# A gated mix of two attentions on one core: the first scores ahead of the last projected tile, and one PSUM layout for both parts

## The chip, the core and the metric

The kernel runs on one core of a Trainium2 chip. The metric is the device time of one execution in microseconds (us). Engines are named as the profile names them: PE (TensorE matmul), PEld (its weight loads), DVE (VectorE), ACT (ScalarE), POOL (GpSimd) and SP (SyncE, which issues nearly all DMAs). All lines (L…) are those of the kernel before, unless the kernel after is named.

## What is computed

With `x` of 2048 rows and 448 columns, 16 heads of 28, and two sets of weights:

```python
g = sigmoid((x * gate_w).sum(-1, keepdims=True))
# A: sliding window, 8 keys, 2 apart, per head
kg = k[:, :, idx_c, :]; vg = v[:, :, idx_c, :]
logits = einsum("bhsd,bhswd->bhsw", q, kg) * scale        # masked, softmax over w
a = (softmax(logits) weighted sum of vg) @ A_wo
# B: full attention, 16 heads
p = softmax(einsum("bhqd,bhkd->bhqk", q, k) * 28 ** -0.5)
b = einsum("bhqk,bhkd->bhqd", p, v) @ B_wo
return g * a + (1 - g) * b
```

All is float32. The kernel splits each matmul operand into a high and a low part and sums three products.

## The kernel before, in words

**Part one, the projections** (from the start to about 252.7 us). 92 tiles, written out in a list, give q, k, v of both attentions. From tile 10 on a tile is summed in two halves of 64 contraction rows, which run side by side on PE, into the two halves of one PSUM tile `PJ[n % 2]` (L289); ACT copies both halves out (L362), POOL adds them (L363). Between the products stand matmuls of another kind, `s1_half` (L155): they work out full score rows, of which DVE keeps only the row maximum (L162), because the softmax of B needs the maximum before its exponentials. Each of tiles 12 to 91 carries four of them, into `PM[0]` and `PM[1]`, and gives four of the 1024 maxima.

**Part two, attention B with attention A beside it** (about 252.7 to 788 us) is a loop of 256 steps: 16 units (4 head groups by 4 blocks of 512 queries) of 16 key tiles. A step does, in this order on PE:

- `scores` (L1016): twelve matmuls for four heads (three products each), in tokens like `"10"` (bank 1, product 0). While maxima are left, three matmuls for maxima stand between them (`s0`, `s1`, `s2`, L144). `s0` goes into `T1`, `s1` and `s2` into a pair of banks. DVE reduces `T1` to one maximum and the pair to two (L148).
- ACT takes the exponential of two heads at a time, two instructions a step (L1044).
- `do_av` (L992) of the **previous** step: four matmuls of exponentials with V into `av` (L995), summed over the 16 key tiles of a unit.

The order on each engine is the order in which the program is written, with its waits set by a recording layer from the tiles that instructions read and write. One step later than a unit's last `do_av`, `fin_copy` (L852) has ACT copy `av` out to `osb` (L854). In step 0 no `do_av` is due, and two matmuls on idle data stand in its place (L1116).

Into the steps go, by lists with due steps and costs (L685 to L755), the instructions of attention A: POOL does its products, DVE its reductions (L626, L637, L647) and transposes (L674), ACT eight exponentials (`L`, L642). When a unit's 64 maxima are there, `max_parts` (DVE, ACT, POOL; L172), two steps later `max_turn` (DVE, L186) and `max_store` (SP) put them into DRAM, from where `load_q` (L119) reads them as two more rows of the next queries.

**The end.** After step 234 no maxima are left, and 92 pieces of the output projection (L838) are spread over steps 235 to 255; the rest follows.

**PSUM.** Part one holds four tiles `PS[0..3]` of two banks each (r0 to r3; the numbers 128, 132, 136, 140 in the rows below). At the change to part two this pool is closed and three tiles T0 to T2 of two banks, and two separate tiles of one bank, `T1` and `av`, are taken in the same place (L532 to L537).

Of the kernel before, what the change touches and what calls it, by code (L numbers as in the profile page):

```python
# [25 lines left out]
def gated_mix_kernel(ctx: ExitStack, tc: tile.TileContext, xT, xn, gw, wA, wB, woAB, out):  # L26
# [24 lines left out]
    tctx = [ExitStack()]  # L51
    PS = [tctx[0].enter_context(tc.tile_pool(name=f"ps{i}", bufs=1, space=bass.MemoryType.PSUM)).tile(
        [128, 2, 512], F32, name=f"r{i}") for i in range(4)]
    PJ, PM = PS[0:2], PS[2:4]
    T = []

    def banks(n):
        for i in range(n):
            pool = ctx.enter_context(tc.tile_pool(name=f"t{i}", bufs=1, space=bass.MemoryType.PSUM))
            T.append(pool.tile([128, 2, 512], F32, name=f"T{i}"))  # L60

# [144 lines left out]
    with tc.tile_pool(name="xp", bufs=1) as xp, tc.tile_pool(name="wp", bufs=2) as wp:  # L206
# [77 lines left out]

        def product(n, p, half, first, last):
# [3 lines left out]
            bank = PS[n % 4][:, 0, :] if half is None else PJ[n % 2][:, half, :]  # L289
# [38 lines left out]

        fini = []
# [9 lines left out]
        def qk_tile(n, nb, rows):  # L339
# [8 lines left out]
            nc.scalar.activation(raw, PJ[n % 2], AF.Copy)  # L348
# [10 lines left out]
        def add_halves(n, dst, gate=None):  # L359
            raw = pair("raw")  # L360
            cols = D + 2 * (gate is not None)
            nc.scalar.activation(raw[:, :, 0:cols], PJ[n % 2][:, :, 0:cols], AF.Copy)  # L362
# [88 lines left out]
        for n, t in enumerate(tiles):  # L451
# [77 lines left out]
    tctx[0].close()  # L529
    pctx.close()  # L530
    pm = ctx.enter_context(tc.tile_pool(name="pm", bufs=8))
    banks(3)  # L532
    RP = T[2], T[0]
    TP = T[1]
    pool = ctx.enter_context(tc.tile_pool(name="psv", bufs=1, space=bass.MemoryType.PSUM))
    T1 = pool.tile([128, 512], F32, name="T1")
    av = pool.tile([128, 512], F32, name="av")  # L537

# [155 lines left out]
    for c in range(8):  # L696
# [28 lines left out]
        for i in range(4):  # L725
            item("dve", c0 + 53 + 0.1 * i, ("t", c, i), 0.43 if c < 7 else 0.35, [(("a", c, W - 1, 1), 1), (("t", c, i - 1), 0)],
# [275 lines left out]
    ALONE = "10 20 30 00 11 21 31 01 12 22 32 02".split()  # L1002
# [13 lines left out]
    def scores(u, kt, cur):  # L1016
# [10 lines left out]
        for tok in WITH if k else ALONE:  # L1027
            if tok[0] == "s":
# [49 lines left out]
    for u in range(NU):  # L1078
        g, b = divmod(u, NB)
        for kt in range(NJ):  # L1080
            st = NJ * u + kt
            if kt == (8 if u < 12 else 12) and u + 1 < NU:
                load_q(u + 1)
# [16 lines left out]
            if finished:  # L1100
# [5 lines left out]
                lag = 2 if v < NU - 1 else 1  # L1106
# [3 lines left out]
            issue("act", st, 0)  # L1110
# [3 lines left out]
            else:  # L1114
                for _ in range(2):
# [68 lines left out]
```

## Time and profile before

| what | value |
|---|---|
| median of 3 runs | 905.44 us (905.26 to 906.26) |
| the profiled execution's own time | 906.4 us |
| its span from first to last instruction | 904.6 us |
| PE busy | 897.4 us (99%) |
| DVE, ACT, POOL busy | 735.3, 646.1, 633.7 us |
| granted TensorE clock | 1.00 |

A row of the timeline reads: start, length, engine, line, operation, tile written and tiles read, how many instructions are merged in it, and in brackets the idle time of the engine ahead of it with what ended that. A row of the groups reads: line, engine, operation, tiles and shapes, count, then busy time and mean of one in ns, then idle time ahead and who ended it. Matmul records start when a matmul enters the array, and their ends are modelled, so PE shows as busy throughout.

### The profile page before, as it was taken

Reading aid. Unit: us, or ns where it says so; the run is one execution under the profiler, and the core shown is the slowest. Engines: PE = TensorE matmul, PEld = TensorE weight load, DVE = VectorE, ACT = ScalarE, POOL = GpSimd, SP = SyncE. Lnnn points to the kernel's source line nnn. Section 1 sums busy time; section 2 is a strip of 40 time slices with the busy share of each in tenths; the row PEclk is TensorE's granted clock in tenths of the full one; section 3 lists DMA queues with packets and bytes.
Section 4 is the critical chain, followed back from the end, with each engine's and each line's share of the span. In section 5 each row is a group of like instructions: output and inputs, shape, how many; then the busy total and the mean of one; then the engine's idle time right before and its main releaser. Section 6 shows DMA issues by size and latency. Waiting matters only on the chain.

```text
span 904.6 us, 20583 instructions
## 1 busy us (share of the span) xinstructions
PE 897.4 (99%) x8334; PEld 534.2 (59%) x8334; DVE 735.3 (81%) x989; ACT 646.1 (71%) x775; POOL 633.7 (70%) x502
## 2 busy tenths in 40 slices
PE   9999999999999999999999999999999999999998
PEld 6899999999944444444444444444444444466667
DVE  6488999999989999999999999999999888610012
ACT  6456434443378898898989889888889898855550
POOL 2489847464479799998989999899999389500100
PEclk9999999999999999999999999999999999999999
DMA  9887403554362341245144421523122413455333
GB/s 269 289 264 194 142 12 84 145 133 121 96 245 65 98 119 54 81 108 130 27 120 122 113 89 42 141 66 79 48 82 55 134 26 103 126 155 146 91 95 102
DMA packets 113838, 104.29 MB, mean 115 GB/s; under 512 B 74628, under 2 KB 82180, under 8 KB 112960
## 3 DMA queue, kind: packets, MB, share of 16 engines
q1 hardware_dynamic: 113600, 102.72, 40.2%
q8 instruction: 65, 1.06, 0.5%
q10 hardware_dynamic: 144, 0.26, 0.1%
q14 instruction: 29, 0.24, 0.1%
HBM read 61.99 MB, written 40.48 MB: 113 GB/s over the span
## 4 chain that ended last, share of the span: by engine, by line
PE 92%; POOL 4%; ACT 1%; DVE 1%; DMA 0%; issue 0%; SPq 0%; ACTq 0%; DVEq 0%; POOLq 0%
PE T L1041 28%; PE av L995 26%; PE r L298 15%; PE T L838 8%; PE r L293 8%; PE r L144 5%; PE T L144 4%; POOL oat L670 1%; POOL prod L665 1%; ACT P L1044 1%; DMA raw<-in_wB 0%; POOL prod L616 0%; DVE MX L148 0%; SPq L220 0%; POOL prod L621 0%
## 5 line engine op out<-in xcount | busy, mean ns | idle before, releaser
L1044 ACT ACTIVATE P<-T 128x1024 f32<-128x1024 f32 x512 | 497.2, 1025 | 92.2 <-PE T L1041 91.0
L148 DVE TENSOR_REDUCE MX<-T 128x1 f32<-128x512 f32 x470 | 440.1, 952 | 22.4 <-PE T L144 10.3
L995 PE MATMUL av<-P,V 128*32 128x512 f32 x2048 | 272.7, 605 | 0.4 <-ACT osb L854 0.3
L1041 PEld LDWEIGHTS T<-QH,KH 30*128 30x128 f32 x1024 | 90.6, 181 | 221.4 <-ACT P L1044 196.9
L144 PE MATMUL T<-KH,QP 28*128 28x512 f32 x704 | 219.4, 454 | 0.3 <-DVE MX L162 0.3
L162 DVE TENSOR_REDUCE MX<-r 128x2 f32<-128x1024 f32 x160 | 192.6, 1220 | 24.7 <-PE r L144 23.1
L1041 PE MATMUL T<-QH,KH 30*128 30x512 f32 x1024 | 210.9, 489 | 1.0 <-DVE MX L148 0.8
L1041 PE MATMUL T<-QH,KL 28*128 28x512 f32 x1024 | 185.8, 397 | 0.0
L1041 PE MATMUL T<-QL,KH 28*128 28x512 f32 x1024 | 182.9, 392 | 0.0
L616 POOL TENSOR_TENSOR prod<-qt,kt 128x896 f32<-128x896 f32 x64 | 135.5, 2120 | 0.2
L362 ACT ACTIVATE raw<-r 128x896 f32<-128x896 f32 (+1 forms) x64 | 58.9, 920 | 97.9 <-PE r L298 96.6
L670 POOL TENSOR_TENSOR oat<-oat,prod 128x896 f32<-128x896 f32 x56 | 118.2, 2110 | 2.7
L144 PEld LDWEIGHTS T<-KH,QP 28*128 28x128 f32 x704 | 86.0, 181 | 27.6 <-ACT P L1044 20.9
L363 POOL TENSOR_TENSOR ast<-raw 128x448 f32<-128x448 f32 x48 | 55.4, 1154 | 58.2 <-ACT raw L362 45.8
L665 POOL TENSOR_TENSOR prod<-vt,L 128x896 f32<-128x896 f32 x56 | 95.5, 1705 | 0.6
L1041 PEld LDWEIGHTS T<-QL,KH 28*128 28x128 f32 x1024 | 93.2, 184 | 0.0
L1041 PEld LDWEIGHTS T<-QH,KL 28*128 28x128 f32 x1024 | 91.7, 183 | 1.0
L144 PE MATMUL r<-KH,QP 64*128 64x512 f32 x320 | 86.7, 390 | 0.0
L995 PEld LDWEIGHTS av<-P,V 128*32 128x32 f32 x2048 | 40.3, 108 | 78.1 <-issue 73.1
L298 PE MATMUL r<-wh,xh 64*128 64x448 f32 (+1 forms) x512 | 85.4, 362 | 0.0
L298 PE MATMUL r<-wh,xl 64*128 64x448 f32 (+1 forms) x384 | 70.0, 363 | 0.0
L298 PE MATMUL r<-wl,xh 64*128 64x448 f32 (+1 forms) x448 | 66.1, 367 | 0.0
(120 smaller groups left out, 1038.1 us busy)
## 6 DMA issues: line engine op xcount, KB each, us to landing
a_scr<-ast SPq DMA_DIRECT2D x24, 448.0 KB
qk_hi<-qkh SPq DMA_DIRECT2D x24, 256.0 KB
qk_lo<-qkh SPq DMA_DIRECT2D x24, 256.0 KB
rbc<-rs SPq DMA_DIRECT2D x60, 64.0 KB
QP<-qk_hi SPq DMA_DIRECT2D x64, 56.0 KB
KL<-qk_lo SPq DMA_DIRECT2D x16, 224.0 KB
QH<-qk_hi SPq DMA_DIRECT2D x64, 56.0 KB
QL<-qk_lo SPq DMA_DIRECT2D x64, 56.0 KB
```

Of the source, the lines that this page charges most:

```text
L144: nc.tensor.matmul(bank, qhis[u][h % 2][r, 128 * qs:128 * qs + 128], KH[u // NB % 3][r, 512 * kc:512 * kc + 512], start=True, stop=True)
L148: r = nc.vector.tensor_reduce(MX[:, n % NMX:n % NMX + k], bank, axis=X, op=ALU.max)
L162: nc.vector.tensor_reduce(m, PM[k], axis=X, op=ALU.max)
L293: nc.tensor.matmul(bank, ws[c][rows, k, t[4]:t[4] + 128], x, start=first, stop=last)
L298: nc.tensor.matmul(bank[:, 0:cols], x, ws[c][rows, k, 0:cols], start=first, stop=last)
L616: nc.gpsimd.tensor_tensor(out=p, in0=qt[c], in1=kvt["k", c % 2][:, HALO - DIL * w:HALO - DIL * w + NJ, :], op=ALU.mult)
L665: nc.gpsimd.tensor_tensor(out=dst, in0=kvt["v", c % 2][:, HALO - DIL * w:HALO - DIL * w + NJ, :].rearrange("p j (h d) -> p j h d", d=DH), ...
L670: nc.gpsimd.tensor_tensor(out=oat[c], in0=oat[c], in1=oat[c, w], op=ALU.add)
L838: writes(bank, nc.tensor.matmul(bank[:, :D], src, wo[c][:, k, :], start=(first and k == ks[0] and i == 0), stop=(last and k == ks[-1] and ...
L995: nc.tensor.matmul(av[32 * h:32 * h + 32, :], V[:, kt, 4 * g + h, :], tiles_[h], start=(kt == 0), stop=(kt == NJ - 1), skip_group_check=True)
L1041: nc.tensor.matmul(bank[a], (KH[g % 3], KH[g % 3], KL[g % 2])[t][r, ks], (qh, ql, qh)[t][r, :], start=(t == 0), stop=(t == 2))
L1044: e = nc.scalar.activation(p, RP[0] if a == "2" else mine, AF.Exp, scale=SCALE).ins
```

## The change

The four tiles `PS[0..3]` now stay for both parts. `RP` is `PS[2]` and `PS[1]`, `TP` is `PS[3]`; **`T1` and `av` are the two halves of `PS[0]`**. The last projected tile (91) goes to `PS[3]` and carries no matmuls for maxima, so that `PS[2]` and `PS[1]` are free for the twelve score matmuls and two exponentials of step 0, which are issued ahead of it (`first_scores`). Four maxima more are left for part two, in steps 1 to 236; the output pieces are spread over steps 237 to 255. Step 0 has no score matmuls, no maxima and no idle matmuls any more. Further: `max_turn` four steps after `max_parts` instead of two; A's transposes of its last two chunks a step later; A's exponentials not in the first three steps of units 0 to 11; the queries of the last unit loaded at the 15th key tile rather than the 13th; a pair of maxima that would wrap around the store `MX` is reduced in two pieces.

```diff
-    tctx = [ExitStack()]
-    PS = [tctx[0].enter_context(tc.tile_pool(name=f"ps{i}", bufs=1, space=bass.MemoryType.PSUM)).tile(
+    PS = [ctx.enter_context(tc.tile_pool(name=f"ps{i}", bufs=1, space=bass.MemoryType.PSUM)).tile(
         [128, 2, 512], F32, name=f"r{i}") for i in range(4)]
     PJ, PM = PS[0:2], PS[2:4]
...
+    RP, TP = (PS[2], PS[1]), PS[3]
+    T1, av = PS[0][:, 0, :], PS[0][:, 1, :]
...
+        def joint(n):
+            return TP if n == len(tiles) - 1 else PJ[n % 2]
...
+        def first_scores():
+            qh, ql = Qs[0]
+            for tok in ALONE:
+                h, t = int(tok[0]), int(tok[1])
+                r = slice(32 * h, 32 * h + (DH + 2 if t == 0 else DH))
+                bank = RP[h in (0, 3)][:, h in (0, 2), :]
+                nc.tensor.matmul(bank, (KH[0], KH[0], KL[0])[t][r, 0:128], (qh, ql, qh)[t][r, :],
+                                 start=(t == 0), stop=(t == 2))
+                if t == 2 and h in (0, 2):
+                    p = pair(f"P{h}")
+                    nc.scalar.activation(p, RP[h == 0], AF.Exp, scale=SCALE)
+                    cur0[(h + 3) % 4], cur0[h] = p[:, 0, :], p[:, 1, :]
...
+            if n == len(tiles) - 1:
+                first_scores()
             if n < FULL:
                 project(n)
             else:
-                project_halves(n, [S1_START <= m < S1_START + 80 for m in (n, n + 1)])
+                project_halves(n, [S1_START <= m < len(tiles) - 1 for m in (n, n + 1)])
...
-    banks(3)
-    RP = T[2], T[0]
-    TP = T[1]
-    pool = ctx.enter_context(tc.tile_pool(name="psv", bufs=1, space=bass.MemoryType.PSUM))
-    T1 = pool.tile([128, 512], F32, name="T1")
-    av = pool.tile([128, 512], F32, name="av")
...
-            item("dve", c0 + 53 + 0.1 * i, ("t", c, i), 0.43 if c < 7 else 0.35, [(("a", c, W - 1, 1), 1), (("t", c, i - 1), 0)],
+            item("dve", c0 + 53 + 0.1 * i, ("t", c, i), 0.43 if c < 7 else 0.35, [(("a", c, W - 1, 1), 2 if c > 5 else 1), (("t", c, i - 1), 0)],
...
                 elif i == 2 and k > 1:
-                    r = s1_max(n + 1, k - 1, other[:, 0:k - 1, :])
+                    whole = (n + 1) % NMX + k - 1 <= NMX
+                    for j in (0,) if whole else (0, 1):
+                        w = slice(j, k - 1 if whole else j + 1)
+                        r = s1_max(n + 1 + j, w.stop - j, other[:, w, :])
                     apart(r, other)
...
-            if kt == (8 if u < 12 else 12) and u + 1 < NU:
+            if kt == (8 if u < 12 else 12 if u < NU - 2 else 14) and u + 1 < NU:
                 load_q(u + 1)
...
-            cur = {}
+            cur = {} if st else cur0
             left = s1e - s1c[0]
-            for a in scores(u, kt, cur):
+            for a in scores(u, kt, cur) if st else ():
...
-                lag = 2 if v < NU - 1 else 1
+                lag = 4 if v < NU - 1 else 1
...
-            issue("act", st, 0)
+            if kt > 2 or u > 11:
+                issue("act", st, 0)
             run("act", st)
             if prev is not None:
                 do_av(prev)
-            else:
-                for _ in range(2):
-                    nc.tensor.matmul(av, KH[0][:, 0:128], KH[0][:, 0:512], start=True, stop=True, skip_group_check=True)
...
-                op_some(st, (92 * (st - OPS[0] + 1) + 20) // 21 - (92 * (st - OPS[0]) + 20) // 21)
+                i, k = st - OPS[0], 256 - OPS[0]
+                op_some(st, (92 * (i + 1) + k - 1) // k - (92 * i + k - 1) // k)
```

Where the instructions stand now is shown at three places. In these rows L298 of before is L297 of after, L144 is L140, L1041 is L1048, L995 is L1000, L1044 is L1051, L854 is L859, L642 is L647.

The first place is PE's queue from the end of tile 90 to step 0. Here `r_132` is `PS[1]`, `r_136` `PS[2]`, `r_140` `PS[3]`; L298 are products of a tile, L144 matmuls for maxima, L1041 scores. Before:

```order
607 L298 MATMUL r_128<-wh_2337,xl_185 128x448 x5
608 L298 MATMUL r_132<-wh_2337,xh_183 128x448 x4
609 L144 MATMUL r_136<-KH_152,QP_155 128x512 x2
610 L298 MATMUL r_132<-wh_2337,xh_183 128x448 x4
611 L298 MATMUL r_132<-wl_2338,xh_183 128x448 x7
612 L298 MATMUL r_132<-wh_2337,xl_187 128x448
613 L144 MATMUL r_140<-KH_152,QP_156 128x512 x2
614 L298 MATMUL r_132<-wh_2337,xl_187 128x448 x5
615 L1041 MATMUL T_3279<-QH,KH_151 128x512 x2
616 L144 MATMUL T_3283<-KH_152,QP_157 128x512
```

The same place after, where L334 are the twelve early scores:

```order
607 L297 MATMUL r_128<-wh_2337,xl_185 128x448 x5
608 L297 MATMUL r_140<-wh_2337,xh_183 128x448
609 L334 MATMUL r_136<-QH,KH_151 128x512 x2
610 L334 MATMUL r_132<-QH,KH_151 128x512 x2
611 L334 MATMUL r_136<-QL,KH_151 128x512 x2
612 L334 MATMUL r_132<-QL,KH_151 128x512 x2
613 L334 MATMUL r_136<-QH,KL_153 128x512 x2
614 L334 MATMUL r_132<-QH,KL_153 128x512 x2
615 L297 MATMUL r_140<-wh_2337,xh_183 128x448 x7
616 L297 MATMUL r_140<-wl_2338,xh_183 128x448 x7
617 L297 MATMUL r_140<-wh_2337,xl_187 128x448 x6
618 L1048 MATMUL r_136<-QH,KH_151 128x512 x2
```

The scores of step 0 moved ahead of tile 91, but for one product of tile 91 (row 608), which the half that ends first still puts in front of them, and which writes `PS[3]`; tile 91's four matmuls for maxima are gone.

The second place is PE's queue in step 17, the one behind a unit's end, with what each instruction waits for (the engines' semaphores). `T_3283` is `T1`; rows L995 are `do_av`. Before:

```order
1135 L144 MATMUL T_3283<-KH_152,QP_158 128x512 [waits DVE_49]
1136 L1041 MATMUL T_3279<-QL,KH_151 128x512 x2
1137 L1041 MATMUL T_3275<-QH,KH_151 128x512 [waits DVE_49]
1138 L1041 MATMUL T_3275<-QH,KH_151 128x512
1139 L1041 MATMUL T_3279<-QH,KL_153 128x512 x2
1140 L1041 MATMUL T_3275<-QL,KH_151 128x512 x2
1141 L144 MATMUL T_3271<-KH_152,QP_157 128x512 [waits Activation_49]
1142 L144 MATMUL T_3271<-KH_152,QP_158 128x512
1143 L1041 MATMUL T_3275<-QH,KL_153 128x512 x2
1144 L995 MATMUL av<-P_3295,V 32x512 [waits Activation_49]
1145 L995 MATMUL av<-P_3294,V 32x512 x2
1146 L995 MATMUL av<-P_3295,V 32x512
```

After, where both `T1` and `av` lie in the tile `r_128`:

```order
1133 L140 MATMUL r_128<-KH_152,QP_157 128x512 [waits Activation_49]
1134 L1048 MATMUL r_136<-QL,KH_151 128x512 x2
1135 L1048 MATMUL r_132<-QH,KH_151 128x512 [waits DVE_49]
1136 L1048 MATMUL r_132<-QH,KH_151 128x512
1137 L1048 MATMUL r_136<-QH,KL_153 128x512 x2
1138 L1048 MATMUL r_132<-QL,KH_151 128x512 x2
1139 L140 MATMUL r_140<-KH_152,QP_158 128x512
1140 L140 MATMUL r_140<-KH_152,QP_157 128x512
1141 L1048 MATMUL r_132<-QH,KL_153 128x512 x2
1142 L1000 MATMUL r_128<-P_3285,V 32x512 [waits DVE_49]
1143 L1000 MATMUL r_128<-P_3285,V 32x512
1144 L1000 MATMUL r_128<-P_3286,V 32x512 x2
```

No instruction moved here, but the waits did. The first `do_av` matmul now waits for DVE: the count it waits for is that of the reduction of `T1` of the same step. This stands in all 236 steps with maxima; before, no `do_av` waited for DVE. And `s0` (row 1133 of after) now waits for ACT's copy `osb` at the 14 unit ends among these steps, where before the first `do_av` matmul did (row 1144 of before).

The third place is ACT's queue around step 48, where the copy `osb` and an exponential of attention A (`L`) met. Before:

```order
266 L1044 ACTIVATE P_3294<-T_3279 128x1024
267 L1044 ACTIVATE P_3295<-T_3271 128x1024
268 L642 ACTIVATE L<-L 128x256
269 L854 ACTIVATE osb<-av 128x512
270 L1044 ACTIVATE P_3296<-T_3279 128x1024
271 L1044 ACTIVATE P_3297<-T_3275 128x1024
```

After:

```order
266 L1051 ACTIVATE P_3285<-r_136 128x1024
267 L1051 ACTIVATE P_3286<-r_140 128x1024
268 L859 ACTIVATE osb<-r_128 128x512
269 L1051 ACTIVATE P_3283<-r_136 128x1024
270 L1051 ACTIVATE P_3284<-r_132 128x1024
271 L915 ACTIVATE onhi<-on 128x512
272 L1051 ACTIVATE P_3285<-r_136 128x1024
273 L1051 ACTIVATE P_3286<-r_140 128x1024
274 L1051 ACTIVATE P_3283<-r_136 128x1024
275 L1051 ACTIVATE P_3284<-r_132 128x1024
276 L647 ACTIVATE L<-L 128x256
```

The exponential of A went three steps back, and two such extra instructions no longer follow each other.

More of the change, by code (lines that the diff above doesn't have):

```diff
@@ L47, in gated_mix_kernel @@
     pp = pctx.enter_context(tc.tile_pool(name="pp", bufs=8))
-    tctx = [ExitStack()]
-    PS = [tctx[0].enter_context(tc.tile_pool(name=f"ps{i}", bufs=1, space=bass.MemoryType.PSUM)).tile(
+    PS = [ctx.enter_context(tc.tile_pool(name=f"ps{i}", bufs=1, space=bass.MemoryType.PSUM)).tile(
         [128, 2, 512], F32, name=f"r{i}") for i in range(4)]
     PJ, PM = PS[0:2], PS[2:4]
[L55 to L60, printed above, removed]
+    RP, TP = (PS[2], PS[1]), PS[3]
+    T1, av = PS[0][:, 0, :], PS[0][:, 1, :]
+    ALONE = "10 20 30 00 11 21 31 01 12 22 32 02".split()
     ident = cp.tile([128, 128], F32, name="ident")
@@ L288, in product @@
             rows = slice(0, 128) if half is None else slice(64 * half, 64 * half + 64)
-            bank = PS[n % 4][:, 0, :] if half is None else PJ[n % 2][:, half, :]
+            bank = PS[n % 4][:, 0, :] if half is None else joint(n)[:, half, :]
             a, c, k = p
@@ L326, in project_halves @@
                         f(*x)
+        def first_scores():
[10 more added lines that the diff above has]
+                    cur0[(h + 3) % 4], cur0[h] = p[:, 0, :], p[:, 1, :]
+        cur0 = {}
         fini = []
@@ L347, in qk_tile @@
             raw = pair("raw")
-            nc.scalar.activation(raw, PJ[n % 2], AF.Copy)
+            nc.scalar.activation(raw, joint(n), AF.Copy)
             r = raw[:, 0, :]
@@ L361, in add_halves @@
             cols = D + 2 * (gate is not None)
-            nc.scalar.activation(raw[:, :, 0:cols], PJ[n % 2][:, :, 0:cols], AF.Copy)
+            nc.scalar.activation(raw[:, :, 0:cols], joint(n)[:, :, 0:cols], AF.Copy)
             nc.gpsimd.tensor_tensor(out=dst, in0=raw[:, 0, 0:D].rearrange("p (c e) -> p c e", e=dst.shape[-1]),
@@ L526, in run @@
             f()
-    tctx[0].close()
     pctx.close()
     pm = ctx.enter_context(tc.tile_pool(name="pm", bufs=8))
-    banks(3)
-    RP = T[2], T[0]
-    TP = T[1]
-    pool = ctx.enter_context(tc.tile_pool(name="psv", bufs=1, space=bass.MemoryType.PSUM))
-    T1 = pool.tile([128, 512], F32, name="T1")
-    av = pool.tile([128, 512], F32, name="av")
     last_read = {}
@@ L1001, in gated_mix_kernel @@
     WITH = "10 20 s0 11 21 30 00 12 22 31 01 s1 s2 32 02".split()
-    ALONE = "10 20 30 00 11 21 31 01 12 22 32 02".split()
     turn = [0]
```

## The prediction

> **What bounds the kernel now.** First the page, for shares and slices:
>
> ```profile
> span 904.6 us, 20583 instructions
> PE 897.4 (99%) x8334; PEld 534.2 (59%) x8334; DVE 735.3 (81%) x989; ACT 646.1 (71%) x775; POOL 633.7 (70%) x502
> DVE  6488999999989999999999999999999888610012
> ACT  6456434443378898898989889888889898855550
> ```
>
> PE is busy throughout, but its ends are modelled, so 99% proves little. DVE is at 9 in the whole of part two, ACT at 8 to 9. So I asked for the groups between 262 and 780 us, the steady part of the step loop:
>
> ```profile
> L1044 ACT ACTIVATE P<-T 128x1024 f32<-128x1024 f32 x458 | 444.9, 1025 | 59.7 <-PE T L1041 58.5
> L148 DVE TENSOR_REDUCE MX<-T 128x2 f32<-128x1024 f32 x229 | 279.9, 1222 | 8.2 <-PE T L1041 2.4 <-PE T L144 0.2
> L626 DVE TENSOR_REDUCE L<-prod 128x8 f32<-128x224 f32 x96 | 33.8, 373 | 0.0
> L626 DVE TENSOR_REDUCE L<-prod 128x16 f32<-128x224 f32 x80 | 28.3, 369 | 0.0
> ```
>
> 458 exponentials, two a step, are 228.5 step lengths from the first to the last start, in 518 us: **2.267 us a step**. ACT waits 58.5 us there, so it isn't the bound. What ends last in a step is read from the timeline of two ordinary steps (some rows of it):
>
> ```profile
> 477.54 0.50 PE L144 MATMUL T<-KH,QP 28*128 28x512 f32 x1
> 478.11 0.69 DVE L148 TENSOR_REDUCE MX<-T 128x1 f32<-128x512 f32 x1 [0.23 <-PE T L144]
> 478.44 0.50 PE L144 MATMUL T<-KH,QP 28*128 28x512 f32 x2
> 478.88 1.07 PE L995 MATMUL av<-P,V 128*32 128x512 f32 x8
> 478.99 1.23 DVE L148 TENSOR_REDUCE MX<-T 128x2 f32<-128x1024 f32 x1 [0.19 <-PE T L1041]
> 479.88 0.49 PE L144 MATMUL T<-KH,QP 28*128 28x512 f32 x1
> 480.13 0.67 DVE L626 TENSOR_REDUCE L<-prod 128x8 f32<-128x224 f32 x2
> 480.27 0.18 PEld L1041 LDWEIGHTS T<-QH,KH 30*128 30x128 f32 x2
> 480.72 1.81 DVE L148 TENSOR_REDUCE MX<-T 128x1 f32<-128x512 f32 x2
> 481.17 1.06 PE L995 MATMUL av<-P,V 128*32 128x512 f32 x8
> 482.17 0.49 PE L144 MATMUL T<-KH,QP 28*128 28x512 f32 x1
> 482.45 0.37 DVE L626 TENSOR_REDUCE L<-prod 128x8 f32<-128x224 f32 x1
> ```
>
> At 477.54, 479.88 and 482.17 PE begins a step with the first scores and `s0`. `do_av` follows at 478.88 and 481.17, and the next step exactly 1.00 us behind its start, both times. So PE sets the pace, with DVE close: the reduction of `T1` starts 0.57 us after `s0` (478.11) when DVE is free, 0.84 us (480.72) when two reductions of attention A stand ahead of it. It ends at 478.80 and at about 481.40. `do_av` started 0.08 us after that end in the one step and **0.23 us before** it in the other; before the change it had no need to care.
>
> **The change part by part.**
>
> *`T1` and `av` in one tile, every step.* The row of PE's queue in the section on the change says that `do_av` now waits for the reduction of `T1` of its own step. PE is in order, so behind the waiting instruction stand the rest of `do_av` and all scores of the next step, its `s0` among them; and DVE's next reduction waits for that `s0`. That closes a loop: `s0` to the reduction's start 0.57, the reduction 0.69, release of PE 0.05 (the pair's reduction ends at 478.99 + 1.23 = 480.22, the weights that wait for it load at 480.27), `do_av` to the next `s0` 1.00. Sum **2.31 us, a floor** under each step with maxima, above today's mean of 2.267. DVE's own loop with two A reductions is 480.72 to 482.45, 1.73, and from the first of them to `T1` again 0.59, in all 2.32; it now adds its delay to PE's directly. I take 2.325, near the floor, because most steps hold at most two such pieces. What stretched the mean of 2.267 (below) is in that mean and not in 2.325.
>
> *The same tile, at a unit's end.* The copy `osb` and what it held up, in step 17:
>
> ```profile
> 291.98 0.49 PE L144 MATMUL T<-KH,QP 28*128 28x512 f32 x1
> 292.52 0.61 ACT L854 ACTIVATE osb<-av 128x512 f32<-128x512 f32 x1
> 293.18 1.06 PE L995 MATMUL av<-P,V 128*32 128x512 f32 x8
> 294.17 0.50 PE L1041 MATMUL T<-QH,KH 30*128 30x512 f32 x2
> ```
>
> The copy ends at 293.13, and `do_av` starts at 293.18. Before, only `do_av` waited for it, and lost next to nothing, since the scores ran meanwhile. Now `s0`, third in the queue, waits: 293.18 instead of 291.98, 1.20 us. The step ahead is about 0.05 longer, so 1.15; the copy can't come sooner, since ACT has the exponentials of the step before in front of it. 14 unit ends lie among the steps with maxima: 14 x 1.15 = **16.1 us**.
>
> *Step 0 ahead of tile 91.* Rows at the change of parts, and one of the chain of work that ended last, from a late step:
>
> ```profile
> 249.70 2.35 DVE L162 TENSOR_REDUCE MX<-r 128x2 f32<-128x1024 f32 x2 [0.23 <-PE r L144]
> 249.90 0.58 PE L298 MATMUL r<-wh,xh 64*128 64x448 f32 x4
> 252.73 0.50 PE L1041 MATMUL T<-QH,KH 30*128 30x512 f32 x2
> 252.84 0.92 ACT L362 ACTIVATE raw<-r 128x896 f32<-128x896 f32 x1 [1.73 <-PE r L298]
> 254.63 0.73 PE L1116 MATMUL av<-KH 128*128 128x512 f32 x2
> 257.81 0.50 PE L1041 MATMUL T<-QH,KH 30*128 30x512 f32 x2
> 806.36 2.63 PE T L838 x12
> 808.99 0.91 PE T L1041 x10
> 809.90 0.99 PE av L995 x8
> ```
>
> Tile 91's products begin at about 249.9, and step 2 at 257.81. After: the one product that stands ahead of the early scores writes `PS[3]`, which DVE reads for tile 90's maxima until 249.70 + 1.22 = 250.92 (the first of the two merged; 1.22 is also the mean of the pair's reduction above); released 250.97. This wait of 1.07 us is new, and the early scores queue behind it. Then 0.1 for the product, 0.91 for twelve scores, and 2.27 for the other 20 products (2.83 for 21 with four maxima matmuls, less about 0.45 for these, less one): step 1 begins at 254.25. Its `s1` needs the copy of tile 91, 0.11 + 0.92 later, 255.28, released 255.33; from `s1` to `do_av` 0.44 (478.44 to 478.88): 255.77, and step 2 at 256.77. That is **1.04 us earlier**. The two idle matmuls (0.73 us) go within it: they stood where PE waited for ACT anyway. The early exponentials run while PE does tile 91.
>
> *Two steps more with maxima.* 235 steps from step 2 on instead of 233, and 19 without instead of 21. One without is 0.91 + 0.99 = 1.90 of PE, plus output pieces, whose sum stays.
>
> *The small edits.* The stalls they go for, from the timeline and the waits:
>
> ```profile
> 261.18 0.21 DVE L186 STREAM_TRANSPOSE nms<-nmt 128x32 f32<-128x32 f32 x1 [0.88 <-POOL nmt L181]
> 705.34 0.45 DVE L674 STREAM_TRANSPOSE oatT<-oat 128x256 f32<-128x256 f32 x1 [0.95 <-POOL oat L670]
> 364.78 0.42 ACT L642 ACTIVATE L<-L 128x256 f32<-128x256 f32 x1
> ```
>
> The later `max_turn` and the later transposes can save at most 0.88 and 0.95; the later exponential at most 0.42 at each of two unit ends: 2.7 in all. In the new loop they save nothing of their own. The wrapped pair costs DVE one more short reduction, some 0.2 us, four times; DVE idles longer than that in a step at the floor. The last queries' loads move two steps back, in SP's queue past loads of the output part:
>
> ```profile
> 786.10 0.27 DVE L174 TENSOR_REDUCE m<-MX 128x16 f32<-128x64 f32 x1
> 796.80 1.10 SPq L101 DMA_DIRECT2D QH<-nm x2
> ```
>
> From the unit's last maxima to the end of the last issue are 11.8 us; three steps without maxima (237 to 239), each 1.90 and some 13 output matmuls of 2.63 / 12 = 0.22, hold some 14. If that cover fails, it costs a microsecond or two once.
>
> *Sum.* Steps: 235 x 2.325 - 233 x 2.267 = 18.2; two steps fewer without maxima -3.8; unit ends +16.1; change of parts -1.0. In all **+29.5**. On the profiled execution's 906.4 (span 904.6) that is 935.9 (934.1); the median of the runs shown is 1.0 below that execution, so **934.9 us**. With the floor of 2.31, 1.08 a unit end and -1.3, the sum is 24.7; with 2.36, 1.25 and -0.5 it is 39.6 (at 2.36 the steps alone give 26.4).
>
> **The rivals.**
>
> *The waits cost nothing (faster).* If the reduction of `T1` were always over 0.05 us before PE is ready for `do_av`, and the copy before `s0`, only the edits would count: -1.0, two steps 2 x (2.267 - 1.90) = +0.7, stalls at most -2.7: 902.4 us. For it: 478.80 against 478.88. Against: 481.40 against 481.17, and the copy that ends 1.15 us after `s0` is due. A rule speaks for it too: the Trainium skill, "PSUM — Partial Sum Buffer", section "PSUM bank collisions raise a hardware error", has two engines collide only in the same bank and quadrant, and says that different banks run clean; the two halves of that tile are two banks. By that rule the chip has no need of the wait, and the time would be this rival's 902.4; no run here shows it, and the wait stands in the program whatever the banks. Chance 0.04.
>
> *Only the unit ends cost.* If the 0.05 to 0.2 us that `do_av` loses came back in the scores behind it: 14 x 1.20 = 16.8, -1.0, +0.7, -2.7: +13.8, 919.2 us. Against it stands the floor, which has nothing in it that could shrink. Chance 0.07.
>
> *DVE and PE take turns badly.* If each step with two A reductions cost their plain durations, 0.69 + 1.22 + 2 x 0.37 = 2.65, and some 80 of the 229 steps hold two (176 of these pieces are in the two rows above, with other kinds beside them): 80 x 0.33 = 26 more, 961 us. The row 480.72 with two reductions in 1.81 shows that they overlap. Chance 0.05.
>
> **How the numbers follow.** Forecast 0.84, the rivals 0.04, 0.07 and 0.05. The predicted time is the forecast's 934.9. The range takes its bounds, 930.1 to 945.0, a little wider on both sides for a step that is off by 0.01 to 0.02: 926 to 948; it leaves out the three rivals. Faster by over 0.2% (1.8 us, about what a measurement of this kernel can tell from none) is the first rival but for its mildest part: 0.035; within it 0.015; slower 0.95.
>
> **What would show it.** In the profile after: a step of 2.31 to 2.36 us between 262 and 780; PE waiting for DVE's `T1` reduction ahead of `do_av` in most of 236 steps; `s0` waiting for `osb` 14 times by 1.1 to 1.2 us; ACT idle for longer; step 2 about 1 us earlier. A step of 2.28 or less would prove the floor wrong, and unit ends as short as other steps the second term.

## The result, and the profile after

The kernel after takes 936.24 us (median of 4 runs, 936.0 to 936.64), the kernel before beside it 905.76 us (4 runs, 905.26 to 906.26): the ratio is 1.0337, with a 95% interval of 1.0324 to 1.0349. The profiled execution of after took 936.19 us, with a span of 934.4 us and a granted clock of 1.00, as before. So the change costs 30.5 us, against +29.5 forecast. In this section L1000 is `do_av`, L140 the matmuls for maxima, L144 their reductions, L1051 the exponentials, L1048 the scores, L859 the copy `osb`, L297 and L334 the products and the early scores.

First the page of after: the span, the busy shares, and of the chain of work that ended last its shares by engine and by line.

```profile
span 934.4 us, 20604 instructions
PE 892.1 (95%) x8332; PEld 522.9 (56%) x8332; DVE 743.9 (80%) x993; ACT 648.1 (69%) x775; POOL 633.6 (68%) x502
PE 67%; DVE 24%; issue 2%; DMA 2%; POOL 2%; SPq 2%; ACT 2%; ACTq 0%; DVEq 0%
PE r L1000 19%; DVE MX L144 19%; PE r L297 14%; PE r L1048 13%; PE r L292 7%; PE r L843 7%; PE r L140 6%; DVE L L631 3%; SPq L97 1%; ACT osb L859 1%; DMA V<-in_xT 1%; DMA onlo<-on_lo 0%; POOL oat L675 0%; POOL prod L621 0%; DVE oatT L679 0%
```

The busy times of all engines are almost what they were; only the span grew. Of the chain, this is the row by engine in the page of before:

```profile
PE 92%; POOL 4%; ACT 1%; DVE 1%; DMA 0%; issue 0%; SPq 0%; ACTq 0%; DVEq 0%; POOLq 0%
```

DVE's share went from 1% to 24%, and `do_av` and DVE's reductions stand side by side with 19% each. That is what a loop through two engines looks like: the chain goes from the one to the other and back in every step.

The waits of after: engine and line, what they waited for, us in total, how often, the longest.

```profile
ACT P L1051 <- PE r L1048: 118.9, 221, 3.4
PEld r L1000 <- DVE MX L144: 109.5, 236, 0.6
DVE MX L144 <- PE r L140: 43.5, 104, 4.2
PEld r L140 <- ACT osb L859: 14.0, 14, 1.0
```

The first weights of `do_av` wait for DVE in all 236 steps with maxima, and `s0` waits for `osb` 14 times: just the two waits that the order of after showed, and as often. DVE and ACT wait for PE in turn. Between 262 and 780 us the group of `T1`'s reduction in before was

```profile
L148 DVE TENSOR_REDUCE MX<-T 128x1 f32<-128x512 f32 x228 | 156.1, 685 | 12.0 <-PE T L144 8.7 <-PE T L1041 1.4
```

and in after the exponentials and that reduction are

```profile
L1051 ACT ACTIVATE P<-r 128x1024 f32<-128x1024 f32 x433 | 420.1, 1022 | 81.2 <-PE r L1048 79.0
L144 DVE TENSOR_REDUCE MX<-r 128x1 f32<-128x512 f32 x225 | 154.5, 688 | 37.2 <-PE r L140 33.1
```

433 exponentials are 216 step lengths in 518 us, 2.398 us a step with the unit ends in it. ACT's idle time has grown from 59.7 to 81.2 us, and that of DVE ahead of `T1`'s reduction from 12.0 to 37.2 us. A stretch of the timeline with the end of unit 6 and the three steps after it:

```profile
483.21 1.06 PE L1000 MATMUL r<-P,V 128*32 128x512 f32 x8
484.20 0.18 PEld L1048 LDWEIGHTS r<-QH,KH 30*128 30x128 f32 x2 [0.84 <-ACT P L1051]
484.75 0.60 ACT L859 ACTIVATE osb<-r 128x512 f32<-128x512 f32 x1
485.41 0.49 PE L140 MATMUL r<-KH,QP 28*128 28x512 f32 x1 [0.71 <-ACT osb L859]
486.69 1.07 PE L1000 MATMUL r<-P,V 128*32 128x512 f32 x8
487.69 0.49 PE L140 MATMUL r<-KH,QP 28*128 28x512 f32 x1
488.23 1.92 DVE L144 TENSOR_REDUCE MX<-r 128x1 f32<-128x512 f32 x2 [0.18 <-PE r L140]
488.98 1.07 PE L1000 MATMUL r<-P,V 128*32 128x512 f32 x8
490.06 0.68 DVE L642 TENSOR_REDUCE lm<-L 128x16 f32<-128x128 f32 x2
490.67 1.80 DVE L144 TENSOR_REDUCE MX<-r 128x1 f32<-128x512 f32 x2
491.39 1.06 PE L1000 MATMUL r<-P,V 128*32 128x512 f32 x8 [0.20 <-DVE MX L144]
```

The loop can be read off: `s0` at 487.69, its reduction 0.54 later, 0.69 long, `do_av` 0.06 behind its end (488.98), and the next step 1.00 behind that. From one `do_av` to the next it is 2.29 us where DVE is free before `s0` is through (486.69 to 488.98), and 2.41 (to 491.39) where two reductions of attention A, 0.68 us together, stand ahead of `T1`'s. At the unit's end the step begins at 484.20, but `s0` starts only at 485.41, 0.06 behind the end of `osb`: 3.48 from `do_av` to `do_av`.

The starts of every second exponential give the step lengths throughout the trace. After has about 2.29 or 2.38 to 2.45 in nearly all ordinary steps, 2.328 in the mean (the 14 steps of units 1 to 13 that do not hold a unit's end); before has 2.259. The two steps at a unit's end are 3.26 and 2.50, 5.77 together, against 4.66 before. The two numbers give nearly the whole window back: 216 x 2.328 + 13 x (5.77 - 2 x 2.328) = 517.3 of 518 us.

Last the change of parts. Before, the last products of tile 90 stood here:

```profile
249.28 0.79 PE L298 MATMUL r<-wh,xl 64*128 64x448 f32 x5
```

After:

```profile
249.47 0.79 PE L297 MATMUL r<-wh,xl 64*128 64x448 f32 x5
251.16 0.47 PE L297 MATMUL r<-wh,xh 64*128 64x448 f32 x1 [0.90 <-DVE MX L158]
251.56 0.51 PE L334 MATMUL r<-QH,KH 30*128 30x512 f32 x4
257.20 0.50 PE L1048 MATMUL r<-QH,KH 30*128 30x512 f32 x2
```

The single product of tile 91 waits for DVE as forecast, and step 2 starts at 257.20. From the last products of tile 90 that is 7.73 us (257.20 - 249.47), and was 8.53 before (257.81 - 249.28): 0.80 earlier.

### The profile page after: what moved, and what is told of

The parts are those of the page before. It is cut to its first block, busy times and chain, and to the rows that moved or that the text cites. A ratio compares the mean times of both kernels' runs of the same rounds, so it can differ in the third digit from the quotient of the medians.

```text
span 934.4 us, 20604 instructions
## 1 busy us (share of the span) xinstructions
PE 892.1 (95%) x8332; PEld 522.9 (56%) x8332; DVE 743.9 (80%) x993; ACT 648.1 (69%) x775; POOL 633.6 (68%) x502
## 4 chain that ended last, share of the span: by engine, by line
PE 67%; DVE 24%; issue 2%; DMA 2%; POOL 2%; SPq 2%; ACT 2%; ACTq 0%; DVEq 0%
PE r L1000 19%; DVE MX L144 19%; PE r L297 14%; PE r L1048 13%; PE r L292 7%; PE r L843 7%; PE r L140 6%; DVE L L631 3%; SPq L97 1%; ACT osb L859 1%; DMA V<-in_xT 1%; DMA onlo<-on_lo 0%; POOL oat L675 0%; POOL prod L621 0%; DVE oatT L679 0%
## 5 line engine op out<-in xcount | busy, mean ns | idle before, releaser
L1051 ACT ACTIVATE P<-r 128x1024 f32<-128x1024 f32 x510 | 494.7, 1022 | 121.3 <-PE r L1048 118.9
L144 DVE TENSOR_REDUCE MX<-r 128x2 f32<-128x1024 f32 (+1 forms) x476 | 445.3, 949 | 49.8 <-PE r L140 43.5
L140 PE MATMUL r<-KH,QP 28*128 28x512 f32 (+1 forms) x1024 | 296.6, 417 | 9.7 <-ACT osb L859 9.6
L1000 PE MATMUL r<-P,V 128*32 128x512 f32 x2048 | 272.7, 605 | 26.0 <-DVE MX L144 10.6
L1048 PEld LDWEIGHTS r<-QH,KH 30*128 30x128 f32 x1020 | 89.2, 181 | 204.4 <-ACT P L1051 197.9
L1048 PE MATMUL r<-QH,KH 30*128 30x512 f32 x1020 | 192.0, 472 | 0.0
L1048 PE MATMUL r<-QL,KH 28*128 28x512 f32 x1020 | 163.8, 396 | 0.0
L1048 PE MATMUL r<-QH,KL 28*128 28x512 f32 x1020 | 163.1, 395 | 0.0
L140 PEld LDWEIGHTS r<-KH,QP 28*128 28x128 f32 (+1 forms) x1024 | 133.7, 183 | 44.4 <-ACT P L1051 24.8
L1000 PEld LDWEIGHTS r<-P,V 128*32 128x32 f32 x2048 | 40.3, 108 | 117.4 <-DVE MX L144 109.5
L1048 PEld LDWEIGHTS r<-QL,KH 28*128 28x128 f32 x1020 | 98.2, 185 | 0.4
L1048 PEld LDWEIGHTS r<-QH,KL 28*128 28x128 f32 x1020 | 95.7, 184 | 1.5
L297 PE MATMUL r<-wh,xh 64*128 64x448 f32 (+1 forms) x512 | 85.2, 363 | 0.9 <-DVE MX L158 0.9
L297 PE MATMUL r<-wh,xl 64*128 64x448 f32 (+1 forms) x384 | 69.4, 363 | 0.0
L297 PEld LDWEIGHTS r<-wh,xh 64*128 64x128 f32 x512 | 64.0, 184 | 3.1 <-DVE MX L158 1.3
L297 PE MATMUL r<-wl,xh 64*128 64x448 f32 (+1 forms) x448 | 65.7, 367 | 0.0
```

Of the source, the lines that this page charges most:

```text
L140: nc.tensor.matmul(bank, qhis[u][h % 2][r, 128 * qs:128 * qs + 128], KH[u // NB % 3][r, 512 * kc:512 * kc + 512], start=True, stop=True)
L144: r = nc.vector.tensor_reduce(MX[:, n % NMX:n % NMX + k], bank, axis=X, op=ALU.max)
L297: nc.tensor.matmul(bank[:, 0:cols], x, ws[c][rows, k, 0:cols], start=first, stop=last)
L1000: nc.tensor.matmul(av[32 * h:32 * h + 32, :], V[:, kt, 4 * g + h, :], tiles_[h], start=(kt == 0), stop=(kt == NJ - 1), skip_group_check=True)
L1048: nc.tensor.matmul(bank[a], (KH[g % 3], KH[g % 3], KL[g % 2])[t][r, ks], (qh, ql, qh)[t][r, :], start=(t == 0), stop=(t == 2))
L1051: e = nc.scalar.activation(p, RP[0] if a == "2" else mine, AF.Exp, scale=SCALE).ins
```

## The experiments

The theory (A): the two waits, which come only from `T1` and `av` being one tile for the recording layer, are the whole loss. Its rivals: the loss lies in the early scores and the moved instructions (B); the two waits hide each other (C); PE falls out of step with DVE and ACT after a wait and loses more behind it (D). The runs of before that go with a kernel have the median 905.98 us for the first three kernels below and for the one with the early scores ahead of the whole tile, and 905.81 us for the four in between; for the last ones it is given there.

### The two halves as tiles of their own

```diff
-    PS = [ctx.enter_context(tc.tile_pool(name=f"ps{i}", ...)).tile([128, 2, 512], F32, ...) for i in range(4)]
+    tctx = ExitStack()
+    PS = [(tctx if i == 0 else ctx).enter_context(...)...  for i in (1, 2, 3, 0)]
+    PS = PS[3:] + PS[:3]
...
-    T1, av = PS[0][:, 0, :], PS[0][:, 1, :]
...
+    tctx.close()
+    pool = ctx.enter_context(tc.tile_pool(name="psv", bufs=1, space=bass.MemoryType.PSUM))
+    T1 = pool.tile([128, 512], F32, name="T1")
+    av = pool.tile([128, 512], F32, name="av")
```

> The kernel after, with nothing changed but the tiles: after part one PS[0] is closed, and T1 and av are two tiles of one bank each in its place, so that neither do_av nor s0 has the other half's reader to wait for. Theory A (the two waits are the whole loss): the time is that of before with the change of parts (-1.0), two more steps with maxima (+0.7) and the stalls that the small edits go for (0 to -2.7), 902.8 to 905.5 us beside 905.8 of before; steps of 2.25 to 2.28 us, unit ends no longer than other steps by more than 0.2 us. Rival B (the loss lies in the early scores or in the moved turns, loads and exponentials, and the waits only show where PE would idle anyway): 925 us or more, steps still above 2.31.

Measured: 906.55 us (11 runs, 904.82 to 907.78), ratio to before 1.0005 (0.9996 to 1.0013). 29.7 us are gone with nothing changed but that `T1` and `av` are two tiles in the place of one (for which the pools are taken in another order). B falls. The steps are 2.251 in the mean, the two at a unit's end 4.68. The groups between 262 and 780 us, and a piece of the timeline:

```profile
L1057 ACT ACTIVATE P<-r 128x1024 f32<-128x1024 f32 x460 | 446.7, 1024 | 57.5 <-PE r L1054 55.4
L145 DVE TENSOR_REDUCE MX<-T 128x1 f32<-128x512 f32 x229 | 156.9, 685 | 11.5 <-PE T L141 9.2 <-PE r L1054 0.9
```

```profile
757.74 0.65 DVE L145 TENSOR_REDUCE MX<-T 128x1 f32<-128x512 f32 x1
758.08 0.63 ACT L921 ACTIVATE onhi<-on 128x512 fp32r<-128x512 f32 x1 [0.45 <-POOL on L917]
758.12 1.06 PE L1006 MATMUL av<-P,V 128*32 128x512 f32 x8
759.67 0.50 PE L1054 MATMUL r<-QH,KH 30*128 30x512 f32 x2 [0.49 <-ACT P L1057]
788.58 0.63 ACT L921 ACTIVATE onhi<-on 128x512 fp32r<-128x512 f32 x1 [1.12 <-POOL on L917]
790.17 0.50 PE L1054 MATMUL r<-QH,KH 30*128 30x512 f32 x4 [1.17 <-ACT P L1057]
```

Here `do_av` starts to write `av` at 758.12, while DVE reads `T1` until 758.39: the two halves are used at once, and the time is that of before. The Trainium skill, "PSUM — Partial Sum Buffer", section "PSUM bank collisions raise a hardware error", says that two engines on different banks run clean, and this trace agrees.

Yet 906.55 is above the 902.8 to 905.5 expected. The other rows show a part of it: ACT's `onhi` (the high part of a unit's output) now waits twice for a product of POOL, two exponentials queue behind it, and PE idles 0.49 and 1.17 us. The steps there are 2.93 and 3.60 us long. In after they are 2.34 and 2.34: a slower loop leaves POOL more time. The two waits did not cause these stalls, they hid them. The first comes with the small edits, as the run with these alone shows below. The second was in before too: `onhi` waited 1.16 us for POOL at 790.38, but in that step, 235, before has no maxima left; the step takes 5.15 us with its output pieces, and the wait cost nothing.

### Each wait put back alone

Two kernels from the one above. In the first, `s0` waits for `osb` again:

```diff
-        nc.scalar.activation(t, av, AF.Copy)
+        gone[:] = [nc.scalar.activation(t, av, AF.Copy).ins]
...
-                    s1_mm(n + i, bank[tok])
+                    w = s1_mm(n + i, bank[tok])
+                    if i == 0 and gone:
+                        tc.add_manual_dep(w.ins, gone.pop().name, ..., reason="wait put in")
```

> e1 with one wait put back: at a unit's end s0 waits for ACT's copy osb of av; do_av waits for no reduction. Theory A: 14 unit ends by 1.10 us (the lengths 3.26 and 2.50 of the two steps at a unit's end in the kernel after, less twice 2.33) to 1.15, so 15.4 to 16.1 us over e1, about 920; ordinary steps stay at 2.25 to 2.28. Rival C (the two waits hide each other: whoever waits at a unit's end has waited for the step anyway): under 8 us over e1. Rival D (PE comes back out of phase with DVE and ACT after each such wait and loses more in the steps behind it): over 20 us over e1.

Measured: 918.17 us (4 runs, 917.9 to 918.34), 11.6 over the kernel with two tiles. Its waits, and its timeline at one unit's end:

```profile
PEld T L141 <- ACT osb L866: 14.5, 14, 1.2
```

```profile
291.30 0.60 ACT L866 ACTIVATE osb<-av 128x512 f32<-128x512 f32 x1
291.96 0.50 PE L141 MATMUL T<-KH,QP 28*128 28x512 f32 x1 [0.69 <-ACT osb L866]
```

The two steps at a unit's end are 5.62 instead of 4.68, so 0.95 x 14 = 13.3 us, somewhat under the 15.4 to 16.1 expected, and ordinary steps stay at 2.25. That only 11.6 are left in the time is the same POOL story: with the later steps of this kernel the two long steps (2.93 and 3.60) are 2.35 and 2.35 again, 1.8 us back. Neither C nor D.

In the second, `do_av` waits for the reduction of `T1` again:

```diff
-                    s1_max(n, 1, T1)
+                    t1r[:] = [s1_max(n, 1, T1)]
...
+            if t1r:
+                tc.add_manual_dep(w.ins, t1r.pop().name, ..., reason="wait put in")
```

> e1 with the other wait put back: do_av waits in each step with maxima for DVE's reduction of T1 of that step; s0 does not wait for osb. Theory A: 222 ordinary steps by 2.33 - 2.267 = 0.06 each, and 14 unit ends that lose nothing of their own: 13 to 15 us over e1, about 918; steps of 2.29 or 2.41 to 2.43 as in the kernel after. With e2 it adds up to the kernel after within 2 us. Rival C (the waits hide each other): e2 and e3 together fall short of the kernel after or go beyond it by over 5 us. Rival B: no more than 3 us over e1.

Measured: 922.32 us (4 runs, 922.24 to 922.87), 15.8 over the kernel with two tiles. Ordinary steps are 2.329 (2.328 in after), unit ends 4.75. Its waits, of the weight loads and of the array itself:

```profile
PEld av L1007 <- DVE MX L145: 101.8, 222, 0.6
PE av L1007 <- DVE MX L145: 13.9, 66, 0.4
```

11.6 and 15.8 are 27.4, and the kernel after lies 29.7 over the kernel with two tiles: 2.3 apart, a little over the 2 expected, and well under the 5 of C. The base holds 1.8 us of stalls behind POOL (2.93 and 3.60 for two steps of 2.35), this kernel 0.6 of them (2.35 and 2.98), the other one and after none. Without them the waits cost 13.4 and 17.0 alone, 30.4, and 31.5 together: they add up within 1.1 us, and C falls. It is not exact to less than that: a step of 2.07 behind each of the two stalls gives some 0.5 us back, a third stall (step 97, below) takes about as much, and part one of the base's profiled execution ended 0.8 us later than in these two.

### One tile in the kernel before

```diff
-    T1 = pool.tile([128, 512], F32, name="T1")
-    av = pool.tile([128, 512], F32, name="av")
+    TA = pool.tile([128, 2, 512], F32, name="TA")
+    T1, av = TA[:, 0, :], TA[:, 1, :]
```

> The kernel before with one edit: T1 and av are the two halves of one tile of two banks instead of two tiles; no early scores, no moved turns, loads or exponentials. Theory A: 219 ordinary steps by 0.06 (13.1) and 14 unit ends by 1.10 to 1.15 (15.4 to 16.1), 28 to 30 us over before, 934 to 936 us; steps of 2.29 and 2.41, unit ends of 3.26 and 2.50. Rival B (the loss comes with the other edits): within 5 us of before.

Measured: 937.93 us (4 runs, 937.71 to 938.87), ratio 1.0357 (1.0343 to 1.0371), 32.1 over before and 1.7 over after. The layout alone does it all, and a little more than the 934 to 936 expected. Beside the trace of before, 30.4 us of it lie in steps 2 to 234 and 0.9 behind them. Two of the stalls that the small edits go for are seen in its timeline:

```profile
261.34 0.21 DVE L186 STREAM_TRANSPOSE nms<-nmt 128x32 f32<-128x32 f32 x1 [0.92 <-POOL nmt L181]
261.48 0.65 DVE L148 TENSOR_REDUCE MX<-TA 128x1 f32<-128x512 f32 x1
262.18 1.07 PE L995 MATMUL TA<-P,V 128*32 128x512 f32 x8 [0.71 <-DVE MX L148]
370.80 0.42 ACT L642 ACTIVATE L<-L 128x256 f32<-128x256 f32 x1
371.10 0.60 ACT L854 ACTIVATE osb<-TA 128x512 f32<-128x512 f32 x1
371.75 0.50 PE L144 MATMUL TA<-KH,QP 28*128 28x512 f32 x1 [1.00 <-ACT osb L854]
```

DVE's `max_turn` waits 0.92 us for POOL, the reduction of `T1` stands behind it, and `do_av` behind that: 0.71 us of PE. And an exponential of attention A stands ahead of `osb`, so that `s0` comes 1.00 late instead of 0.71. Step 3 takes 2.92 us for it, and step 48 3.57 where other unit ends have 3.26. Before had these two stalls as well, in steps of 2.70 and 2.61 us where 2.30 is usual, so they explain little of what was not expected. The larger part is in the ordinary steps: 2.328 against 2.259 in before, 0.07 more and not 0.06.

### The small edits alone

The kernel before with the later turns, the later transposes, the later exponential, the later loads of the last queries and the split pair, as in the diff of the change.

> The kernel before with the small edits alone: max_turn four steps later instead of two, the transposes of the last two chunks a step later, attention A's exponentials out of the first three steps of units 0 to 11, the last queries' loads two steps later, the wrapped pair in two pieces. Theory A: the stalls that they go for were 0.88 + 0.95 + 0.84 us at most, so 0 to 2.7 us under before, likeliest 0.5 to 1.5, 904.3 to 905.3 us. Rival: the exponential that comes later, or the last queries that come later, cost a wait of their own: 1 to 3 us over before.

Measured: 905.32 us (11 runs, 904.83 to 906.1), ratio 0.9995 (0.9986 to 1.0003). That is 0.5 us under before, which is no more than a measurement can be off. The traces show that this is a gain and a loss. The long steps of before are gone: step 3 goes from 2.70 to 2.26 us, steps 48 and 128 from 2.61 to 2.31 and 2.28, step 199 from 3.19 to 2.34. But step 222 goes from 2.34 to 3.32. The waits of `onhi` for POOL, first in before, then here:

```profile
ACT onhi L910 <- POOL on L906: 1.2, 1, 1.2
```

```profile
ACT onhi L910 <- POOL on L906: 2.9, 2, 2.1
```

The 1.2 us of before and 2.05 of the 2.9 us here stand in step 235, which has no maxima in these two kernels and takes 5.15 and 5.14 us. What has come is the wait of 0.84 us in step 222. In POOL's queue a piece of the output weights (`wo`, 755.20 to 756.98) stands ahead of the product there, which in before comes behind it. Which of the small edits moved it was not tried apart. This kernel has no wait between `T1` and `av`, and it has the first of the two stalls of the kernel with two tiles.

### The floor

If a loop sets the step, a shorter loop must make the wait free. In two kernels DVE reduces 256 of the 512 columns of `T1`; half of that maximum's columns is left out. One is the kernel with two tiles, the other the one in which `do_av` waits.

```diff
-s1_max(n, 1, T1)
+s1_max(n, 1, T1[:, 0:256])
```

> Leaves work out: e1 with DVE's reduction of T1 over 256 of its 512 columns. It is the base for the next run. If DVE is no bound in e1, the time is e1's within 3 us; if DVE's queue sets part of the step, up to 235 x 0.1 = 20 us under e1.

> Leaves work out: e3 (do_av waits for the reduction of T1) with that reduction over 256 of 512 columns. Theory A (a loop with a floor): the reduction is about 0.27 to 0.33 us shorter, so the floor falls from 2.31 to about 2.0, below the step that the rest allows, and the wait costs at most 4 us over the run with the half reduction and without the wait, where it cost 13 to 15 with the whole one. Rival (each wait on DVE costs a fixed time, for its semaphore or for PE's restart, whatever the length of the loop): 10 us or more over it.

Measured: 905.26 us without the wait (10 runs, 904.63 to 907.63) and 905.35 with it (10 runs, 904.67 to 907.06): 0.1 us, where the wait cost 15.8 with the whole reduction. First the group of the reduction with the wait, then the waits of the same kernel:

```profile
L145 DVE TENSOR_REDUCE MX<-T 128x1 f32<-128x256 f32 x230 | 96.1, 418 | 12.0 <-PE T L141 10.0
```

```profile
PEld av L1007 <- DVE MX L145: 59.4, 200, 0.6
PE av L1007 <- DVE MX L145: 1.1, 2, 0.8
```

The reduction is 0.27 us shorter, the floor 0.54 + 0.42 + 0.06 + 1.00 = 2.02 instead of 2.29, and 2.02 is below the 2.25 that the rest of the step takes. A fixed price for each wait is ruled out. The waits are worth a second look. The row of the weight loads still shows 200 waits and 59.4 us, and they cost nothing: while they waited, the array still had the scores ahead of them, since PE itself idled only 1.1 us. The row of the array itself (PE) fell from 66 waits and 13.9 us to 2 and 1.1, and that is the one which followed the time.

### The early scores ahead of the whole tile, and what came out then

In after one product of tile 91 stands ahead of the early scores and waits for DVE. In the next kernel, from the one with two tiles, all products of tile 91 stand behind them:

```diff
-                    if l:
+                    if l and (n < len(tiles) - 2 or l[0][0] == n):
```

> e1 with the early scores ahead of all products of tile 91; in e1 and after one product of it stands ahead of them and waits 0.90 us for DVE's reduction of tile 90's maxima in PS[3]. Theory A: the scores run in that wait, so tile 91 and all that follows come 0.8 to 1.1 us earlier than in e1: about 902 to 904.5 us, under before and after. Rival: the next step is set by the exponentials or by the copy of tile 91 in ACT's queue, so the same as e1 within 0.3 us.

Measured: 905.11 us (11 runs, 904.09 to 908.31), ratio 0.9993 (0.9985 to 1.0002). In its trace:

```profile
250.18 0.78 PE L298 MATMUL r<-wh,xl 64*128 64x448 f32 x5
250.89 0.51 PE L335 MATMUL r<-QH,KH 30*128 30x512 f32 x4
251.81 1.09 PE L298 MATMUL r<-wh,xh 64*128 64x448 f32 x8
256.75 0.50 PE L1054 MATMUL r<-QH,KH 30*128 30x512 f32 x2
```

The wait is gone, and step 2 stands 6.57 us (256.75 - 250.18) behind the last products of tile 90, where it was 7.60 in the kernel with two tiles (257.76 - 250.16), 7.73 in after and 8.53 before. So the trace shows 1.0 us, as expected. The time is 1.4 less, which fits within the spread of the runs; that it lies above the 902 to 904.5 expected comes from the base, which was higher than foreseen. Once more, beside the next kernel:

> e6_scores_first once more, on the same chip and in the same rounds as e9, as its base: 904.5 to 905.7 us.

It took 905.08 us (11 runs). The next kernel takes up the two stalls behind POOL; `onhi` of units 12 and 13 is issued a step later:

```diff
-        l = {NU - 3: (1, 2, 6, 7, 9, 12, 13, 15), ...
+        l = {NU - 4: (1, 3, 6, 8, 12, 16, 17, 19), NU - 3: (1, 2, 6, 7, 9, 13, 14, 15), ...
```

> e6_scores_first with the high part of the normalized output (ACT's onhi) of units 12 and 13 one step later, and what follows it with it. In the trace of e1 ACT waited there 0.45 and 1.12 us for POOL's product, and PE 0.49 and 1.17 us for the exponentials queued behind that wait; the steps there are 2.93 and 3.60 us long, in e6 2.98 and 3.27. Theory: these two steps become 2.3 or less, and 0.7 + 1.0 us go, so 1.2 to 1.7 under e6, about 903.5 to 904 us, the lowest of all here and 0.2% under before. Rival: POOL's lateness only moves on, to the low part and the stores behind it, and the last output pieces wait for them: the same as e6 within 0.5 us.

Measured: 904.11 us (11 runs, 903.47 to 906.73), ratio to its runs of before (905.83) 0.9982 (0.9973 to 0.9991). 1.0 us less than the same kernel without it, a little under what was expected: the step at unit 13's end is still 2.69, for another reason. In its timeline:

```profile
756.59 1.09 SPq L98 DMA_DIRECT2D QH<-nm  x2
759.09 0.50 PE L1054 MATMUL r<-QH,KH 30*128 30x512 f32 x2 [0.49 <-DMA QH<-nm]
```

The maxima of unit 14 are loaded too late now: `max_turn` comes four steps after `max_parts` instead of two. The exponentials' wait had hidden this: in the kernel without this change the same scores waited 0.51 us for the exponentials (758.84). So the last kernel gives unit 14 its two steps back:

```diff
-                lag = 4 if v < NU - 1 else 1
+                lag = 4 if v < NU - 2 else 2 if v < NU - 1 else 1
```

> e9_later_high_part with the turn of unit 14's maxima two steps after their parts again, as in before, instead of four. In the trace of e9 the first scores of unit 14 waited 0.49 us for the DMA of its maxima into QH, at the step that is 2.69 us long; the DMA was issued 2.5 us before that. Theory: the store of the maxima comes some 4.5 us earlier, this wait goes, the step becomes 2.3, and the time is 0.3 to 0.5 us under e9 (903.6 to 903.8), which is less than runs can tell, so the step's length decides. Rival: the scores there wait for the exponentials in any case, which come as late as in e6: the step stays above 2.6.

Measured: 903.87 us (11 runs, 903.48 to 905.52), ratio to its runs of before (905.91) 0.998 (0.9971 to 0.9989). The step is 2.35, so the rival falls; the 0.24 us in the medians is less than runs can tell. This version is faster than both kernels: 2.0 us under before, 32 under after.

One more stall stands in the kernels with two tiles where no wait slows the loop, this last one included. In step 97 a reduction of attention A (`L637`) waits for POOL's product, 0.59 us in the first of these kernels and 1.51 in the last, the reductions of maxima queue behind it on DVE, and PE's scores behind those. The step takes 2.78 and 3.69 us there, where before has 2.33, the kernel with `s0` waiting 2.36, and the kernel with the small edits alone 2.34. Why POOL is late there is open.

## Why the prediction came out right

- **What bounds the kernel.** That the step is set by PE's queue with DVE close behind was the reading on which all else stood. It held: with the wait the loop through DVE sets the step, without it DVE's reduction can be 0.27 us shorter and the time changes by 1.3 us (906.55 to 905.26), within the spread of these runs.
- **`do_av` waits for `T1`, every step.** Right in mechanism, shown three ways (taken away, put back alone, made free by a shorter reduction). The forecast's floor of 2.31 was a little high: its parts measure 0.54 + 0.69 + 0.06 + 1.00 = 2.29. The step of 2.325 was right in the mean, 2.328, but not as put: not "near the floor" throughout, but at 2.29 with steps of 2.41 between, where DVE has two other reductions first. The term was too small by two: 13.6 forecast, 15.8 measured, because the step of 2.267 from which it was counted was a mean over unit ends too. Ordinary steps of before are 2.259, and 2.251 without the waits.
- **`s0` waits for `osb`, at unit ends.** Right in mechanism and in count (14). The step that failed is "Before, only `do_av` waited for it, and lost next to nothing": the two steps at a unit's end took 4.66 before, 0.14 more than two ordinary ones. The weights of `do_av` waited 5.0 us for `osb` at the 14 unit ends of before, PE itself idled only 0.4 us behind it, so how much of the 0.14 is this wait stays open. So not 1.15 but about 1.0 was added each time: 14 x 0.99 = 13.9 (936.24 - 922.32), where 16.1 was forecast. What was put into the one term was missing in the other, and the sum, 29.7 for both, equals the forecast's 13.6 + 16.1 = 29.7. That it does so to the tenth is luck: without the stalls of the kernel with two tiles the two waits cost 31.5.
- **The change of parts.** Forecast -1.04, measured -0.80. The single product was released as put, 1.69 us behind the last products of tile 90 (251.16 - 249.47; forecast 250.97 - 249.28). Mis-sized was the product itself: 0.40 us from its start to the early scores (251.16 to 251.56), taken as 0.1.
- **Two more steps, and the small edits.** Forecast +0.7 and nothing. What is left when the waits are gone, with the change of parts in it, is +0.6 (906.55 - 905.98; the interval of the ratio makes it -0.4 to +1.2) against -0.3. Not foreseen were the stalls behind POOL, which the waits hide: one comes with the small edits (step 222), one was in before at no cost and shows now that step 235 has maxima too, and one stands in step 97. "In the new loop they save nothing of their own" was wrong: the kernel with one tile and without these edits is 1.7 us slower than after, and the early scores (-0.8) and the two more steps (+0.7), which it lacks, nearly cancel. That the rest is the edits' is argued from the two places shown; the edits were measured alone only without the waits (-0.5), where a gain and a new stall nearly cancel.
- **The rivals.** "The waits cost nothing" is refuted by the wait put back alone (+15.8). Its number of 902.4 for the kernel without the waits was too low as well: that kernel takes 906.55, and it took three more edits to come to 903.87. "Only the unit ends cost" would be the 918.17 of the kernel with that wait alone, and "DVE and PE take turns badly" fails on the steps: with two reductions of attention A in the way they are 2.41, not 2.65. These reductions start at 490.06, 0.08 us behind the first scores of the step (489.98), and most of their 0.68 us falls in the 0.54 in which DVE would wait for `s0` in any case.
- **What would show it.** Step, count of both waits, ACT's idle time: as listed. The unit's `s0` was said to wait 1.1 to 1.2 us; in the trace its weights wait 1.0, and its start is 1.21 behind that of the step.

## What to carry to other kernels

Where a recording layer sets the waits, the tile is the unit of dependence: two buffers with different readers want tiles of their own, even if they lie in different banks and would never meet. Before sharing one, list for each instruction what it would newly wait for, and look whether that closes a loop through the queues of two engines; the loop's length against the present step, not the number of waits, says what it costs. And when a wait is taken away, look in the new trace for the one that it had been hiding: here first POOL's product, then a load of maxima. A small edit that seems neutral can be a gain and a new stall of like size; the step lengths of both traces tell them apart.

## What the runs showed of the hardware

A reduction of `T1` from PSUM took 418 ns for 256 columns and 685 for 512, the pair of banks 1223 for 1024: some 1.05 ns a column and 0.15 us besides. From its end to the dependent weight load it was 0.05 to 0.06 us. Part one up to tile 90 is the same in the eight kernels here that have two tiles and the other edits of after. In their nine profiled executions (one kernel ran twice) the last products of tile 90 stood at 249.16 to 249.55 us five times and at 250.07 to 250.18 four times: two groups at least 0.5 us apart, and the instructions of part one alone don't decide between them. Why is open.

The runs of these kernels spread by up to 4 us, and one reason is seen in the profiled execution of the kernel with the shorter reduction and without the wait, which took 907.63 us, the longest of its ten. From 476.0 to 478.2 us its granted clock was 0.53, and from there to 480.0 0.63; before and behind that it was 1.00. The step in this stretch, 98, took 3.88 us, where it took 2.13 to 2.36 in the others.
